# Local and global attention, then routed experts: the scores of a query block from one product of 160 columns on a reordered key buffer

## The chip, the cores and the metric

The kernel runs on one core of a Trainium2 chip. The metric is the device time of one execution in microseconds (us); lower is better. The core has TensorE (PE in the profile: matrix products, with weight loads, PEld, that overlap them), VectorE (DVE), ScalarE (ACT), GpSimd (POOL) and SyncE (SP). GpSimd and SyncE also issue DMAs, each in the order of its own program. Operands lie in SBUF, products land in PSUM, and a DMA moves data between DRAM and SBUF or within them.

## The reference

Batch 8, 8 heads, 512 local positions, 32 global ones, head size 64. A local query sees the 32 global keys and the local keys at most 32 positions away; a global query sees all 544 keys. The result, as 4352 tokens of 512, goes through eight experts, mixed by weights that are balanced in eight rounds.

```python
s_g = scale * np.matmul(q_g, k_all.transpose(0, 1, 3, 2))
out_g = np.matmul(sm(s_g), v_all)
s_ll = scale * np.matmul(q_l, k_l.transpose(0, 1, 3, 2))
mask = np.abs(pos[:, None] - pos[None, :]) <= window        # window = 32
s_ll = np.where(mask, s_ll, -1000000000.0)
s_lg = scale * np.matmul(q_l, k_g.transpose(0, 1, 3, 2))
a_l = sm(np.concatenate([s_lg, s_ll], axis=-1))
out_l = np.matmul(a_l, np.concatenate([v_g, v_l], axis=2))
...
for e in range(E):
    out += P[:, e:e + 1] * (np.maximum(x @ w1[e], 0.0) @ w2[e])
```

## The kernel before

The order of all instructions is written out by hand: each engine executes what the program gives it, in that order, and waits where an operand or a buffer is not ready.

**Units and steps.** A unit n is a pair of heads of one batch (n = 4 b + hp, 32 units). The loop over s (L516) runs 34 steps and works on several units at once. In step s stand, in this order: f1 (first-layer products of experts 0 and 1, `ph`, L475), st_B(s, 0), in even steps st_G1, st_D1(s-1), in odd steps st_G2, f2 (second layer, `py`, L489), st_D2, st_B(s, 1), two f1, st_B(s, 2), st_A(s+1), st_E(s-1), in odd steps st_G3, f2, st_G3n, every fourth step logits, f1. Up to step 6 the order differs a little, the expert products begin in step 5, and in steps 1 to 4 keep_busy (L505) puts products in that nobody reads. TensorE so has attention and expert products mixed in one stream.

**st_A** (L297) transposes the keys and queries of a pair of heads into two PSUM tiles (`pk`, `pq`, L305). VectorE copies the keys in natural order to kTe[n % 4] behind 32 zero columns (L307). ScalarE copies the queries to a block-diagonal tile, qbd (L314, two copies); the first six units (n < NPL) use a plain tile, qpl, instead.

**st_B** (L317) forms the scores of blocks of 64 queries for both heads at once: one product with 128 local keys (L337: 64 queries and 32 keys on each side) and one with the 32 global keys, kgT (L339), into 160 columns of a PSUM tile `sc`. VectorE adds the mask and takes the row extremum (L344), ScalarE the exponential (L347) into Pu.

**st_D1** and **st_D2** transpose the weights (ptw L354, tgx L364 and L368) and copy them out (pw by VectorE, pg and xT by ScalarE). **st_E** (L375) multiplies with the values: va and vb hold the local values at two offsets of 64 rows, vgz the global ones, four times, each for one place of the block in a group of four. VectorE divides (L392, L393).

**G1 to G3n** do the global queries, four heads at a time: G1 (L398) scores against the 512 local keys in kTe, in two products of 480 and 32 columns (because of where kTe ends), and against kgT, `sg`; G3 (L425) multiplies the weights with vb and, in a fifth product, with vgn, which holds the global values in its last 32 rows (L433). G3 of batch b runs in steps 4 b + 3 and 4 b + 5.

**Values.** load_v lets GpSimd load vg (to DRAM, L170), va (L171, L174) and a piece of vb. For the first two batches GpSimd copies va to vb (`part`); later, three DMAs on SP do (L191 to L193). load_vz (L159) then issues on SP four DMAs for vgz and one for vgn (L162) of the batch, from vg; vgz and vgn have two buffers each. For batch 0 load_vz stands ahead of step 0, for batch 1 in step 2 (L546), later in `move`. The wait for vg stands in the first of these DMAs; SP issues nothing behind it until it passes.

**PSUM.** `ph` and `py` share two buffers (ps_mm), `sc`, `pq` and `pl` two (ps_sc), the transposes and `pog` two (ps_tr), `po` and `sg` one (ps_po). The result of the second layer goes from `py` to yst by ScalarE (L492) and, when four are there, to DRAM by SP (L496).

After the loop come the balancing of the mixing weights, with expert products between, and experts 2 to 7 by a scheme of seven products for eight (L810, L908).

Of the kernel before, what the change touches and what calls it, by code (L numbers as in the profile page):

```python
# [23 lines left out]
def kernel(  # L24
# [31 lines left out]
    KW = P  # L56
    SW = KW + Sg
    VW = Dh + 1
    assert (B, H, Sl, Dh, Sg) == (8, 8, 512, 64, 32) and D == H * Dh and F % P == 0
    scale = 1.0 / float(Dh) ** 0.5  # L60

# [66 lines left out]
    with ExitStack() as att:  # L128
# [5 lines left out]
        ps_po = att.enter_context(tc.tile_pool(name="ps_po", bufs=1, space=PSUM))  # L134

        qpl = [att_c.tile([P, Sl], FP16, name=f"qpl{i}") for i in range(2)]
        mask = att_c.tile([P, 3, SW], FP32)
        kgT = att_c.tile([P, HP, B * Sg], FP16)
        qgT = att_c.tile([P, HP, B * Sg], FP16)
        qbd = [att_c.tile([P, NHB, P], FP16, name=f"qbd{i}") for i in range(2)]  # L140
        kTe = [att_c.tile([P, W + Sl + W], FP16, name=f"kTe{i}") for i in range(4)]
        vgr = [att_c.tile([P, 4 * H * VW], FP16, name=f"vgz{i}") for i in range(2)]
        vgz = [t.rearrange("p (a h v) -> p a h v", a=4, h=H) for t in vgr]
        vgn = [att_c.tile([P, H, VW], FP16, name=f"vgn{i}") for i in range(2)]
        own = att_c.tile([P, 4], FP16)
        vab = [(att_c.tile([P, NJ, H, VW], FP16, name=f"va{i}"),
                att_c.tile([P, NJ, H, VW], FP16, name=f"vb{i}")) for i in range(2)]
        xgn = [att_c.tile([P, D], FP16, name=f"xgn{i}") for i in range(2)]
        vg16 = [dscr.tile([Sg, H, Dh], FP16, name=f"vg16_{b}") for b in range(B)]

        staged = {}

# [6 lines left out]
        def load_vz(b):  # L159
            for i in range(4):  # L160
                nc.sync.dma_start(out=vgz[b % 2][i:P:4, i, :, 0:Dh], in_=vg16[b])
            nc.sync.dma_start(out=vgn[b % 2][P - Sg : P, :, 0:Dh], in_=vg16[b])  # L162

        def load_v(b):
            va, vb = vab[b % 2]
            vz = vgz[b % 2]
            src = v_l[b].rearrange("h s d -> s h d")

            def first():
                nc.gpsimd.dma_start(out=vg16[b], in_=v_g[b].rearrange("h g d -> g h d"))  # L170
                nc.gpsimd.dma_start(out=va[W:P, 0, :, 0:Dh], in_=src[0:96])  # L171

            def mid(j):
                nc.gpsimd.dma_start(out=va[:, j, :, 0:Dh], in_=src[P * j - W : P * j + 96])  # L174

            def last():
                nc.gpsimd.dma_start(out=vb[HB : HB + W, NJ - 1, :, 0:Dh], in_=src[Sl - W : Sl])

            def part(eng, lo):
                if lo:  # L180
                    eng.tensor_copy(out=vb[96:P, NJ - 1], in_=va[W : 2 * W, 0])
                    eng.tensor_copy(out=vb[0:HB, 0:2], in_=va[HB:P, 0:2])
                    eng.tensor_copy(out=vb[0:HB, 2:NJ], in_=va[HB:P, 2:NJ])
                else:
                    eng.tensor_copy(out=vb[HB:P, 0:2], in_=va[0:HB, 1:3])
                    eng.tensor_copy(out=vb[HB:P, 2], in_=va[0:HB, 3])

            def move():
                if b < 2:
                    return part  # L190
                nc.sync.dma_start(out=vb[96:P, NJ - 1], in_=va[W : 2 * W, 0])  # L191
                nc.sync.dma_start(out=vb[0:HB, :], in_=va[HB:P, :])
                nc.sync.dma_start(out=vb[HB:P, 0 : NJ - 1], in_=va[0:HB, 1:NJ])  # L193
                if b > 1:
                    load_vz(b)

            return [first] + [lambda j=j: mid(j) for j in range(1, NJ)] + [last, move]

# [61 lines left out]
        nc.scalar.activation(out=ones_f[:, 0:1], in_=ones_f[:, 0:1], func=AF.Exp, scale=0.0)  # L260
        nc.vector.memset(mask, 0.0)
        for t in (kTe[0], kTe[2], kTe[3]):
            nc.vector.memset(t[:, 0:W], 0.0)
            nc.vector.memset(t[:, W + Sl :], 0.0)

        def clear(i, eng):
            va, vb = vab[i]
# [4 lines left out]
        def clear_z(i, eng):  # L272
            eng.memset(vgr[i].bitcast(mybir.dt.uint32), 0)
            eng.tensor_copy(out=vgz[i][:, :, :, Dh], in_=own.unsqueeze(2).to_broadcast([P, 4, H]))
            eng.memset(vgn[i][0 : P - Sg], 0.0)
            eng.memset(vgn[i][P - Sg : P, :, Dh:VW], 1.0)

        clear(0, nc.vector)
        clear(1, nc.vector)
# [17 lines left out]
        def st_A(n):  # L297
            b, hp = divmod(n, HP)
            qs, ks = staged[b]
            qb, kt = qbd[n % 2], kTe[n % 4]  # L300
            pt = [ps_tr.tile([P, Sl], FP16, tag="tr", name="pk"), ps_sc.tile([P, Sl], FP16, tag="sc", name="pq")]
            for t, src in enumerate((ks, qs)):
                for so in range(NJ):
                    for a in range(2):
                        nc.tensor.transpose(pt[t][HB * a : HB * (a + 1), P * so : P * (so + 1)],  # L305
                                            src[:, 2 * hp + a, so, :], identity)
            nc.vector.tensor_copy(out=kt[:, W : W + Sl].rearrange("c (p s) -> c p s", s=NJ),  # L307
                                  in_=pt[0].rearrange("c (s p) -> c p s", s=NJ))
            if n < NPL:
                nc.scalar.copy(out=qpl[n % 2].rearrange("c (p s) -> c p s", s=NJ), in_=pt[1].rearrange("c (s p) -> c p s", s=NJ))  # L310
                return
            for a in range(2):
                r = slice(HB * a, HB * (a + 1))
                nc.scalar.copy(out=qb[r, :, HB * a : HB * (a + 1)].rearrange("c i (p s) -> c i p s", s=NJ),  # L314
                               in_=pt[1][r].rearrange("c (s i p) -> c i p s", s=NJ, i=NHB))

        def st_B(n, part):  # L317
# [10 lines left out]
            for ii in range(ni):  # L328
                i = i0 + ii
                if n < NPL:  # L330
                    for c0, c1, kk in ((0, KW, kt[:, HB * i : HB * i + KW]), (KW, SW, kgT[:, hp, Sg * b : Sg * (b + 1)])):
                        for a in range(2):
                            r = slice(HB * a, HB * (a + 1))
                            nc.tensor.matmul(sc[r, SW * ii + c0 : SW * ii + c1], qpl[n % 2][r, HB * i : HB * (i + 1)],
                                             kk[r], start=True, stop=True)
                    continue
                nc.tensor.matmul(sc[:, SW * ii : SW * ii + KW], qb[:, i, :],  # L337
                                 kt[:, HB * i : HB * i + KW], start=True, stop=True)
                nc.tensor.matmul(sc[:, SW * ii + KW : SW * (ii + 1)], qb[:, i, :],  # L339
                                 kgT[:, hp, Sg * b : Sg * (b + 1)], start=True, stop=True)  # L340
            for ii in range(ni):
                i = i0 + ii
                mi = 0 if i == 0 else (2 if i == NHB - 1 else 1)
                nc.vector.tensor_tensor_reduce(  # L344
                    out=ms[:, ii, :], in0=sc[:, SW * ii : SW * (ii + 1)], in1=mask[:, mi, :],
                    scale=-scale, scalar=BIG, op0=ALU.add, op1=ALU.min, accum_out=d["mx"][:, i : i + 1])
# [51 lines left out]
        def st_G1(b, g):  # L398
            n0 = HP * b + 2 * g
            gc = slice(Sg * b, Sg * (b + 1))  # L400
            sg = ps_po.tile([P, 2 * 512], FP32, tag="po")
            for c0, c1, k0 in ((0, Sl - W, 2 * W), (Sl - W, Sl, W), (Sl, S, None)):
                for hh in range(4):
                    pr, a = divmod(hh, 2)
                    r = slice(HB * a, HB * (a + 1))
                    rhs = kgT[r, 2 * g + pr, gc] if k0 is None else kTe[(n0 + pr) % 4][r, k0 : k0 + c1 - c0]
                    nc.tensor.matmul(sg[W * hh : W * (hh + 1), c0:c1], qgT[r, 2 * g + pr, gc], rhs, start=True, stop=True)  # L407
            m2 = att_wk.tile([P, 2], FP32, tag="m2")
            nc.vector.reduce_max(out=m2[:, 0:1], in_=sg[:, 0:S], axis=AX.X)
# [15 lines left out]
        def st_G3(b, g):  # L425
            pgs = gs.pop((b, g))
            va, vb = vab[b % 2]
            po = ps_tr.tile([P, 512], FP32, tag="tr", name="pog")
            for t in range(5):
                for par in range(2):  # L430
                    r, h0 = slice(HB * par, HB * (par + 1)), 4 * g + 2 * par
                    rhs = vb[:, t, h0 : h0 + 2, :] if t < NJ else vgn[b % 2][:, h0 : h0 + 2, :]
                    nc.tensor.matmul(po[r, 0 : 2 * VW], pgs[:, t, r], rhs, start=(t == 0), stop=(t == 4))  # L433
            gs[(b, g)] = po

# [74 lines left out]
        nc.vector.tensor_copy(out=mask[:, 2, 0:KW], in_=mask[:, 1, 0:KW])  # L510
        nc.vector.memset(mask[:, 0, 0:W], NEG)
        nc.vector.memset(mask[:, 2, 3 * W : KW], NEG)
        st_A(0)
        unread(2, 256)
        first_keys()
        for s in range(NU + 2):  # L516
# [41 lines left out]
            if s >= 6:  # L558
                k, hf = divmod(s - 6, 2)
                if k >= 1:  # L560
                    l2 = [((k - 1) % 2, (k - 1) // 2, 2 * hf + i) for i in range(2)]
            n1 = n2 = 0

            def f1(eng):
# [59 lines left out]
                st_G3n(gb, gg)  # L624
            if s >= 6 and (s - 6) % 4 == 0:
                logits(NJ * ((s - 6) // 4), NJ, ps_sc, "sc")
            if s == 8:
                transpose_g(1, "kgs")
                transpose_g(1, "qgs")
# [10 lines left out]

        def sk_max0():
            nc.vector.reduce_max(out=red[:, 0:1], in_=lg, axis=AX.XY)
            dg = att_wk.tile([P, P], FP32, tag="dg", bufs=1)
            nc.vector.tensor_scalar(out=dg, in0=identity, scalar1=red[:, 0:1], scalar2=None, op0=ALU.mult)
            pm = ps_po.tile([P, P], FP32, tag="po")
            nc.tensor.matmul(pm, ones_f, dg, start=True, stop=True)
# [443 lines left out]
```

## Time and profile before

| what | value |
|---|---|
| time, median of 3 runs | 998.37 us (997.82 to 999.82) |
| the profiled execution's own time | 998.93 us |
| its span, first to last instruction | 997.2 us |
| TensorE busy | 982.5 us, 99% of the span |
| VectorE, ScalarE, GpSimd busy | 767.2, 655.5, 301.7 us |
| granted TensorE clock, mean | 0.998 |
| scores of local blocks, one product with local and one with global keys each | 208 pairs in full width (units 6 to 31), 55 and 27 ns from start to start |
| one step of the loop from step 8 on | about 10.2 us |

All times in the views are microseconds from the span's start, durations of single instructions ns where said. A line of a timeline gives start, length, engine, line of the kernel, operation, destination and source, and in brackets idle time of the engine before it with what ended it. Merged lines (x8) cover several instructions, from the first start to the last end. SPq and POOL lines with DMA_DIRECT2D are issues; the time to landing is told apart. Ends of matmuls are modelled and overlap; their starts tell the rate.

### The profile page before, as it was taken

The numbers are of one execution on the slowest core, as the hardware profiler recorded it, in microseconds if no ns is written. First come the engines' busy times: TensorE is split into PE (matmuls) and PEld (weight loads), VectorE is DVE, ScalarE is ACT, GpSimd is POOL, SyncE is SP. The second block draws the span as 40 slices with busy tenths as digits, with TensorE's granted clock in tenths as the row PEclk, the third lists the DMA queues.
The fourth block names the chain that finished last, engine by engine and source line by source line (L and its number), as shares of the span: only waits on it lengthen the run. The fifth ranks groups of instructions, "written<-read, shape, count | busy, mean of one in ns | idle before, by whom it ended". The sixth has DMA issues, their size and how long they took to land.

```text
span 997.2 us, 22451 instructions
## 1 busy us (share of the span) xinstructions
PE 982.5 (99%) x8868; PEld 641.0 (64%) x8868; DVE 767.2 (77%) x1858; ACT 655.5 (66%) x1342; POOL 301.7 (30%) x364
## 2 busy tenths in 40 slices
PE   7899999999999999999999999999999999999998
PEld 4566566656665555666666666676767676776764
DVE  7866665666653755889999888997899999888885
ACT  6888888888884566765555555557765555555551
POOL 9748887888850102111111111111111111100000
PEclk9999999999999999999999999999999999999999
DMA  9999999999952387554543333575664543123043
GB/s 167 186 156 199 239 206 221 222 200 222 234 144 85 108 241 169 161 147 121 122 107 74 75 75 74 128 214 129 165 148 117 117 96 66 53 65 74 2 106 127
DMA packets 138058, 138.68 MB, mean 139 GB/s; under 512 B 56608, under 2 KB 110048, under 8 KB 135904
## 3 DMA queue, kind: packets, MB, share of 16 engines
q0 software_dynamic: 105696, 87.32, 49.6%
q1 hardware_dynamic: 31696, 49.60, 15.5%
q8 instruction: 69, 1.13, 0.5%
q10 hardware_dynamic: 560, 0.33, 0.1%
q14 instruction: 37, 0.30, 0.1%
HBM read 144.46 MB, written 39.58 MB: 185 GB/s over the span
## 4 chain that ended last, share of the span: by engine, by line
PE 94%; POOL 3%; DMA 1%; DVE 1%; issue 0%; SPq 0%; ACT 0%; POOLq 0%; DVEq 0%
PE z L810 30%; PE pa L908 18%; PE py L489 12%; PE ph L475 12%; PE pb L908 9%; PE pc L908 4%; PE po L388 1%; PE ptw L354 1%; PE zp L879 1%; PE sc L337 1%; DMA vgz<-vg 1%; PE pk L305 1%; PE tgx L364 1%; PE pq L305 1%; PE sg L407 0%; POOL va L174 0%
## 5 line engine op out<-in xcount | busy, mean ns | idle before, releaser
L810 PEld LDWEIGHTS <-hs 128*128 128x128 f16 x2264 | 220.7, 98 | 91.8 <-DVE hs L806 0.4
L810 PE MATMUL z<-w2e,hs 128*128 128x256 f16 x1304 | 195.6, 273 | 0.0
L810 PE MATMUL z<-v,hs 128*128 128x256 f16 x960 | 144.0, 273 | 0.0
L475 PE MATMUL ph<-xT,w1e 128*128 128x512 f16 (+1 forms) x576 | 129.3, 367 | 0.6 <-ACT xT L372 0.6
L347 ACT ACTIVATE Pu<-ms,mx 128x160 f16<-128x160 f32 x256 | 120.1, 636 | 13.3 <-DVE mx L344 10.4
L489 PE MATMUL py<-w2e,hT 128*128 128x512 f16 x544 | 128.2, 379 | 0.0
L831 ACT COPY z<-z 128x256 f32<-128x256 f32 x98 | 35.0, 357 | 141.7 <-PE z L810 141.7
L908 PEld LDWEIGHTS <-w1e 128*128 128x128 f16 x960 | 87.1, 98 | 51.6 <-issue 1.0
L908 PE MATMUL pa<-t,s 128*128 128x512 f16 x384 | 114.2, 379 | 0.0
L726 POOL DMA_DIRECT2D w1e<-in_moe_w_dram x24 | 17.5, 734 | 297.5 <-PE pa L908 220.4
L344 DVE CUSTOM_DVE_ANT_0 ms<-sc,mask 128x160 f32<-128x160 f32 x256 | 70.2, 320 | 46.6 <-ACT yst L492 30.0
L844 DVE SCALAR_TENSOR_TENSOR oy<-z,lg,oy 128x512 f32<-128x512 f32 x128 | 95.8, 749 | 7.6 <-ACT oy L849 5.1
L806 DVE TENSOR_TENSOR hs<-hs 128x512 f16<-128x512 f16 x224 | 94.9, 424 | 8.2
L912 DVE CUSTOM_DVE_ANT_0 hx<-pb,s 128x512 f16<-128x512 f32 x96 | 65.9, 687 | 36.4 <-ACT s L942 30.2
L726 POOL DMA_DIRECT2D w2e<-in_moe_w_dram x24 | 19.8, 833 | 243.6 <-PE z L810 214.2
L928 ACT ACTIVATE hs<-pa 128x512 f16<-128x512 f32 x96 | 57.2, 596 | 47.0 <-PE pa L908 46.9
L475 PEld LDWEIGHTS <-w1e 128*128 128x128 f16 x576 | 53.4, 98 | 52.9
L912 DVE CUSTOM_DVE_ANT_0 hs<-pb,s 128x512 f16<-128x512 f32 x96 | 65.9, 686 | 24.1 <-ACT s L942 23.7
L908 PEld LDWEIGHTS <-s 128*128 128x128 f16 x720 | 65.6, 98 | 28.5 <-issue 0.3
L489 PEld LDWEIGHTS <-hT 128*128 128x128 f16 x544 | 49.8, 98 | 51.9
L480 DVE TENSOR_SCALAR hT<-ph 128x512 f16<-128x512 f32 x58 | 40.1, 692 | 55.1 <-PE ph L475 55.0
L478 ACT ACTIVATE hT<-ph 128x512 f16<-128x512 f32 (+1 forms) x86 | 50.6, 588 | 28.8 <-PE ph L475 28.4
(197 smaller groups left out, 1971.0 us busy)
## 6 DMA issues: line engine op xcount, KB each, us to landing
ys<-yd SPq DMA_DIRECT2D x68, 256.0 KB, 3.2
yd<-yst SPq DMA_DIRECT2D x16, 1024.0 KB, 5.9
pw<-in_moe_w_dram POOLq DMA_DIRECT2D x24, 512.0 KB, 10.1
kept<-psum POOLq DMA_DIRECT2D x24, 512.0 KB, 5.3
s<-kept POOLq DMA_DIRECT2D x12, 768.0 KB, 8.9
v<-kept POOLq DMA_DIRECT2D x12, 768.0 KB, 8.9
w1e<-in_moe_w_dram POOLq DMA_DIRECT2D x12, 512.0 KB, 5.3
w2e<-in_moe_w_dram POOLq DMA_DIRECT2D x12, 512.0 KB, 6.7
```

The costliest lines, as they stand in the source:

```text
L344: nc.vector.tensor_tensor_reduce(out=ms[:, ii, :], in0=sc[:, SW * ii : SW * (ii + 1)], in1=mask[:, mi, :], scale=-scale, scalar=BIG, op0=A ...
L347: nc.scalar.activation(out=d["Pu"][:, i // 4, :, i % 4], in_=ms[:, ii, :], func=AF.Exp, scale=-1.0, bias=d["mx"][:, i : i + 1])
L475: nc.tensor.matmul(ph[:, 0:n], wts[e][0][:, dk, P * fm : P * (fm + 1)], xT[:, dk, c0 : c0 + n], start=(dk == 0), stop=(dk == DP - 1))
L478: nc.scalar.activation(out=hT[:, fm, 0:n], in_=ph[:, 0:n], func=AF.Relu)
L480: nc.vector.tensor_scalar(out=hT[:, fm, 0:n], in0=ph[:, 0:n], scalar1=0.0, scalar2=None, op0=ALU.max)
L489: nc.tensor.matmul(py, hT[:, fk, P * c : P * (c + 1)], wts[e][1][:, fk, :], start=(fk == 0), stop=(fk == FT - 1))
L806: nc.vector.tensor_tensor(out=o, in0=x, in1=y, op=op)
L810: nc.tensor.matmul(o, lhs[:, fk, :], rhs[:, fk, :], start=(first and fk == 0), stop=(fk == HF - 1), skip_group_check=True)
L844: nc.vector.scalar_tensor_tensor(out=o, in0=z, scalar=p, in1=o, op0=ALU.mult, op1=ALU.add)
L908: nc.tensor.matmul(o, lhs[:, dk, P * f : P * (f + 1)], rhs[:, dk], start=(first and n == 0 and dk == 0), stop=(dk == HD - 1), skip_group_c ...
L912: nc.vector._custom_dve(TENSOR_ADD_SAT, out=self.to(i, j), in0=self.of(ps), in1=self.of(s), s0=BIG, s1=0.0)
L928: nc.scalar.activation(out=self.to(1, 0), in_=self.of(self.pa), func=AF.Relu)
```

## The change

kTe becomes 24 chunks of 32 columns. From unit 6 on the keys stand in it in another order: for each group r of two blocks five chunks, with the odd-numbered chunks of keys, the even-numbered ones and, in the fifth, a copy of the global keys, such that the five chunks of an even block lie at every second chunk and those of an odd block side by side. VectorE writes this from PSUM in three copies in place of one (the last doubles the first chunk of keys at the end, where an odd block reads it and the mask hides it), and ScalarE copies the global keys in (k_global), ahead of the copies of the queries. st_B then needs one product of 160 columns; an odd block's keys come in the order 1, 3, 2, 4, so there is a permuted mask, and vb is loaded in that order. For the first two batches vb stays natural (GpSimd's copies), and the odd blocks of units 6 and 7 keep two products. st_G1 takes all local keys in one product from batch 2 on.

vgn becomes a single tile. Its load leaves load_vz: SP gets it in step 4 b + 2 of each batch, batch 0 too, behind what the step has put on SP's queue before. The four-DMA part of load_vz stays. The permuted masks are made by VectorE in step 7. dg loses its own buffer.

```diff
-        kTe = [att_c.tile([P, W + Sl + W], FP16, name=f"kTe{i}") for i in range(4)]
+        kTe = [att_c.tile([P, KC * W], FP16, name=f"kTe{i}") for i in range(4)]
-        vgn = [att_c.tile([P, H, VW], FP16, name=f"vgn{i}") for i in range(2)]
+        vgn = att_c.tile([P, H, VW], FP16)
+        def natural(b):
+            return b < 2
+        def k_block(n, i):
+            kt, r = kTe[n % 4], i // 2 * 5 * W
+            if i % 2:
+                return kt[:, r + 4 * W : r + 9 * W]
+            return kt[:, r : r + 9 * W].rearrange("c (k w) -> c k w", w=W)[:, 0:9:2]
+        def k_natural(n, i):
+            r = (i // 2 * 5 + 4) * W
+            return kTe[n % 4][:, r : r + 4 * W].rearrange("c (y x w) -> c x y w", x=2, w=W)
+        def k_global(n):
+            b, hp = divmod(n, HP)
+            kg = kTe[n % 4][:, 4 * W : 24 * W].rearrange("c (r k w) -> c r k w", k=5, w=W)[:, :, 4]
+            nc.scalar.copy(out=kg, in_=kgT[:, hp, Sg * b : Sg * (b + 1)].unsqueeze(1).to_broadcast([P, NJ, Sg]))
...
         def load_vz(b):
             for i in range(4):
                 nc.sync.dma_start(out=vgz[b % 2][i:P:4, i, :, 0:Dh], in_=vg16[b])
-            nc.sync.dma_start(out=vgn[b % 2][P - Sg : P, :, 0:Dh], in_=vg16[b])
...
-                nc.sync.dma_start(out=vb[0:HB, :], in_=va[HB:P, :])
-                nc.sync.dma_start(out=vb[HB:P, 0 : NJ - 1], in_=va[0:HB, 1:NJ])
+                nc.sync.dma_start(out=vb[0:W, :], in_=va[HB : HB + W, :])
+                nc.sync.dma_start(out=vb[HB : HB + W, :], in_=va[HB + W : P, :])
+                nc.sync.dma_start(out=vb[W:HB, 0 : NJ - 1], in_=va[0:W, 1:NJ])
+                nc.sync.dma_start(out=vb[HB + W : P, 0 : NJ - 1], in_=va[W:HB, 1:NJ])
...
-            nc.vector.tensor_copy(out=kt[:, W : W + Sl].rearrange("c (p s) -> c p s", s=NJ),
-                                  in_=pt[0].rearrange("c (s p) -> c p s", s=NJ))
+            kp = kt[:, W : W + Sl].rearrange("c (p s) -> c p s", s=NJ)
             if n < NPL:
+                nc.vector.tensor_copy(out=kp, in_=pt[0].rearrange("c (s p) -> c p s", s=NJ))
...
+            ko = pt[0].rearrange("c (s r h o p) -> c o r h p s", s=NJ, r=4, h=2, o=2)
+            for o in range(2):
+                kd = kt[:, (2 + 2 * o) * W : (22 + 2 * o) * W].rearrange("c (r k p s) -> c r k p s", r=4, k=5, s=NJ)
+                kd = kd[:, :, 0:2] if o else kd[:, :, 0:5:4]
+                nc.vector.tensor_copy(out=kd, in_=ko[:, o])
+            nc.vector.tensor_copy(out=kt[:, 22 * W : 23 * W].rearrange("c (p s) -> c p s", s=NJ), in_=ko[:, 0, 0, 0])
+            k_global(n)
...
-                nc.tensor.matmul(sc[:, SW * ii : SW * ii + KW], qb[:, i, :],
-                                 kt[:, HB * i : HB * i + KW], start=True, stop=True)
-                nc.tensor.matmul(sc[:, SW * ii + KW : SW * (ii + 1)], qb[:, i, :],
-                                 kgT[:, hp, Sg * b : Sg * (b + 1)], start=True, stop=True)
+                elif natural(b) and i % 2:
...
+                else:
+                    nc.tensor.matmul(sc[:, SW * ii : SW * (ii + 1)], qb[:, i, :], k_block(n, i), start=True, stop=True)
...
+            else:
+                cols = [(0, Sl, None)]
...
+            if s < NU and hp == 2:
+                nc.sync.dma_start(out=vgn[P - Sg : P, :, 0:Dh], in_=vg16[b])
...
+            if s == 7:
+                permuted_masks()
```

More of the change, by code (lines that the diff above doesn't have):

```diff
@@ L58 @@
     VW = Dh + 1
+    KC = 24
     assert (B, H, Sl, Dh, Sg) == (8, 8, 512, 64, 32) and D == H * Dh and F % P == 0
@@ L136 @@
         qpl = [att_c.tile([P, Sl], FP16, name=f"qpl{i}") for i in range(2)]
-        mask = att_c.tile([P, 3, SW], FP32)
+        mask = att_c.tile([P, 4, SW], FP32)
         kgT = att_c.tile([P, HP, B * Sg], FP16)
@@ L176, in last @@
             def last():
-                nc.gpsimd.dma_start(out=vb[HB : HB + W, NJ - 1, :, 0:Dh], in_=src[Sl - W : Sl])
+                r = HB if natural(b) else W
+                nc.gpsimd.dma_start(out=vb[r : r + W, NJ - 1, :, 0:Dh], in_=src[Sl - W : Sl])
             def part(eng, lo):
@@ L188, in move @@
             def move():
-                if b < 2:
+                if natural(b):
                     return part
                 nc.sync.dma_start(out=vb[96:P, NJ - 1], in_=va[W : 2 * W, 0])
-                nc.sync.dma_start(out=vb[0:HB, :], in_=va[HB:P, :])
-                nc.sync.dma_start(out=vb[HB:P, 0 : NJ - 1], in_=va[0:HB, 1:NJ])
-                if b > 1:
-                    load_vz(b)
+                nc.sync.dma_start(out=vb[0:W, :], in_=va[HB : HB + W, :])
+                nc.sync.dma_start(out=vb[HB : HB + W, :], in_=va[HB + W : P, :])
+                nc.sync.dma_start(out=vb[W:HB, 0 : NJ - 1], in_=va[0:W, 1:NJ])
+                nc.sync.dma_start(out=vb[HB + W : P, 0 : NJ - 1], in_=va[W:HB, 1:NJ])
+                load_vz(b)
             return [first] + [lambda j=j: mid(j) for j in range(1, NJ)] + [last, move]
@@ L262 @@
         for t in (kTe[0], kTe[2], kTe[3]):
-            nc.vector.memset(t[:, 0:W], 0.0)
-            nc.vector.memset(t[:, W + Sl :], 0.0)
+            nc.vector.memset(t[:, 0 : W], 0.0)
+            nc.vector.memset(t[:, W + Sl : 2 * W + Sl], 0.0)
         def clear(i, eng):
@@ L274, in clear_z @@
             eng.tensor_copy(out=vgz[i][:, :, :, Dh], in_=own.unsqueeze(2).to_broadcast([P, 4, H]))
-            eng.memset(vgn[i][0 : P - Sg], 0.0)
-            eng.memset(vgn[i][P - Sg : P, :, Dh:VW], 1.0)
+            if i == 0:
+                eng.memset(vgn[0 : P - Sg], 0.0)
+                eng.memset(vgn[P - Sg : P, :, Dh:VW], 1.0)
         clear(0, nc.vector)
@@ L335, in st_B @@
                                              kk[r], start=True, stop=True)
-                    continue
-                nc.tensor.matmul(sc[:, SW * ii : SW * ii + KW], qb[:, i, :],
-                                 kt[:, HB * i : HB * i + KW], start=True, stop=True)
-                nc.tensor.matmul(sc[:, SW * ii + KW : SW * (ii + 1)], qb[:, i, :],
-                                 kgT[:, hp, Sg * b : Sg * (b + 1)], start=True, stop=True)
+                elif natural(b) and i % 2:
+                    nc.tensor.matmul(sc[:, SW * ii : SW * ii + KW], qb[:, i, :], k_natural(n, i), start=True, stop=True)
+                    nc.tensor.matmul(sc[:, SW * ii + KW : SW * (ii + 1)], qb[:, i, :],
+                                     kgT[:, hp, Sg * b : Sg * (b + 1)], start=True, stop=True)
+                else:
+                    nc.tensor.matmul(sc[:, SW * ii : SW * (ii + 1)], qb[:, i, :], k_block(n, i), start=True, stop=True)
             for ii in range(ni):
                 i = i0 + ii
-                mi = 0 if i == 0 else (2 if i == NHB - 1 else 1)
+                mi = (0 if i == 0 else 2 if i == NHB - 1 else 1) if i % 2 == 0 or natural(b) else 2 if i == NHB - 1 else 3
                 nc.vector.tensor_tensor_reduce(
@@ L401, in st_G1 @@
             sg = ps_po.tile([P, 2 * 512], FP32, tag="po")
-            for c0, c1, k0 in ((0, Sl - W, 2 * W), (Sl - W, Sl, W), (Sl, S, None)):
+            if n0 < NPL:
+                cols = [(0, Sl - W, 2 * W), (Sl - W, Sl, W)]
+            elif natural(b):
+                cols = [(P * t, P * (t + 1), 2 * t + 1) for t in range(NJ)]
+            else:
+                cols = [(0, Sl, None)]
+            for c0, c1, k0 in cols + [(Sl, S, None)]:
                 for hh in range(4):
                     pr, a = divmod(hh, 2)
-                    r = slice(HB * a, HB * (a + 1))
-                    rhs = kgT[r, 2 * g + pr, gc] if k0 is None else kTe[(n0 + pr) % 4][r, k0 : k0 + c1 - c0]
+                    n, r = n0 + pr, slice(HB * a, HB * (a + 1))
+                    if c0 == Sl:
+                        rhs = kgT[r, 2 * g + pr, gc]
+                    elif n < NPL:
+                        rhs = kTe[n % 4][r, k0 : k0 + c1 - c0]
+                    elif natural(b):
+                        rhs = k_natural(n, k0)[r]
+                    else:
+                        rhs = kTe[n % 4][r, 4 * W : 24 * W].rearrange("c (t k) -> c t k", t=NJ)[:, :, 0:P]
                     nc.tensor.matmul(sg[W * hh : W * (hh + 1), c0:c1], qgT[r, 2 * g + pr, gc], rhs, start=True, stop=True)
@@ L431, in st_G3 @@
                     r, h0 = slice(HB * par, HB * (par + 1)), 4 * g + 2 * par
-                    rhs = vb[:, t, h0 : h0 + 2, :] if t < NJ else vgn[b % 2][:, h0 : h0 + 2, :]
+                    rhs = vb[:, t, h0 : h0 + 2, :] if t < NJ else vgn[:, h0 : h0 + 2, :]
                     nc.tensor.matmul(po[r, 0 : 2 * VW], pgs[:, t, r], rhs, start=(t == 0), stop=(t == 4))
@@ L512, with permuted_masks @@
         nc.vector.memset(mask[:, 2, 3 * W : KW], NEG)
+        def permuted_masks():
+            for i in (3, 2):
+                nc.vector.tensor_copy(out=mask[:, i, 0:KW].rearrange("q (y x w) -> q x y w", x=2, w=W),
+                                      in_=mask[:, 1, 0:KW].rearrange("q (x y w) -> q x y w", x=2, w=W))
+            nc.vector.memset(mask[:, 2, 3 * W : KW], NEG)
         st_A(0)
@@ L642, in sk_max0 @@
             nc.vector.reduce_max(out=red[:, 0:1], in_=lg, axis=AX.XY)
-            dg = att_wk.tile([P, P], FP32, tag="dg", bufs=1)
+            dg = att_wk.tile([P, 3, SW], FP32, tag="ms", name="dg")[:, 0, 0:P]
             nc.vector.tensor_scalar(out=dg, in0=identity, scalar1=red[:, 0:1], scalar2=None, op0=ALU.mult)
```

## The prediction

> **What bounds the kernel now.** I read the busy rows first, then the stretches of 25 us, then the timelines of each engine, in one steady step and in the first 50 us. The page and the stretches (columns: stretch, its length, busy time of PE, weight loads, VectorE, ScalarE, GpSimd, granted clock, DMA share, GB/s):
>
> ```profile
> PE 982.5 (99%) x8868; PEld 641.0 (64%) x8868; DVE 767.2 (77%) x1858; ACT 655.5 (66%) x1342; POOL 301.7 (30%) x364
> ...
> 0.00:25.00 25.00, 18.96 (x315) 11.98 (x317) 19.12 (x93) 17.09 (x37) 23.73 (x40) 0.93 1.42 167
> 25.00:50.00 25.00, 21.77 (x424) 14.80 (x423) 20.06 (x84) 21.99 (x51) 17.65 (x26) 1.00 1.55 186
> ...
> 200.00:225.00 25.00, 25.00 (x307) 14.90 (x305) 15.68 (x63) 20.64 (x45) 20.76 (x22) 1.00 1.17 202
> ```
>
> From about 53 us on TensorE never stops: every ns taken from its stream comes off the end, and every stall put into it is added. Only the first 50 us have holes, and there the chain of waits runs through GpSimd and its DMAs. So two places count: the steady step (some 10.2 us, steps 8 to 31) and the first steps.
>
> **The steady step.** Starts of matmuls on TensorE (start, length, engine, line, what), in step 21 and, the last two lines, in step 20:
>
> ```profile
> 192.40 0.22 PE L337 MATMUL sc<-kTe,qbd 128*128 128x128 f16 x1
> 192.45 0.18 PE L339 MATMUL sc<-kgT,qbd 128*128 128x32 f16 x1
> 192.48 0.22 PE L337 MATMUL sc<-kTe,qbd 128*128 128x128 f16 x1
> ...
> 187.74 0.18 PE L339 MATMUL sc<-kgT,qbd 128*128 128x32 f16 x1
> 187.85 0.41 PE L305 MATMUL pk<-identity,ks 128*64 128x128 f16 x8
> ```
>
> From start to start 128 columns take 55 ns and 32 columns 27 ns, 82 ns a block (eight 512-column products take 1.73 us, 216 ns each). One product of 160 columns: 216 x 160/512 = 68 ns, so 14 ns less. The last two lines show the exception: before work of another shape (transposes of 64 columns, or sg) the 32 columns take 107 ns; that is a drain, and a longer last product should wait it out just the same, 55 + 107 against 68 + about 94. I count nothing there (0 to 14 ns). Blocks that become one product: 26 units (6 to 31) x 8, less the 4 odd ones of units 6 and 7, is 200; 36 of them stand before such a change of shape (23 before the transposes of keys, 13 before sg). 164 x 14 ns = 2.3 us. The scores of the global queries (L407) go from 480 + 32 + 32 columns to 512 + 32: the four that run side by side take 217 instead of 204 ns and a group of 28 ns goes, 15 ns x 12 = 0.2 us. **TensorE: -2.5 us** (2.3 to 3.0).
>
> VectorE: one key copy becomes three. Copies of 512 strided fp16 from PSUM (L307) hold the engine 0.60 us, the 160-column reductions of L344 0.24, so about 1.04 ns a column plus 0.07; 256 + 256 + 32 columns make 0.77, so +0.17 us a step. After it VectorE idles 0.8 to 1.3 us before hT (L480) or lg (L464) in each steady step: hidden. If that cover were gone the hT copy would hold a ph buffer, 0.17 x 24 = 4 us. Units 6 and 7 and the permuted masks (two copies and a memset, 0.41 + 0.34 + 0.09 us by L509 to L512) fall into steps 5 to 7, where VectorE is nearly full: +0.4 us (0 to 1).
>
> ScalarE: the copy of global keys stands between Pu and qbd, and behind it wait the two qbd copies and yst:
>
> ```profile
> 189.53 1.28 ACT L314 COPY qbd<-pq 64x512 f16<-64x512 f16 x2
> 190.87 0.59 ACT L492 COPY yst<-py 128x512 f32<-128x512 f32 x1
> ...
> 190.67 1.89 PE L475 MATMUL ph<-xT,w1e 128*128 128x512 f16 x8
> ```
>
> The second ph tile of the last line (start 190.67 + 0.86 = 191.53) takes the PSUM buffer that yst frees at 191.46: 0.07 us of room, in every step. In front of yst there is 0.33 us in odd steps; in even ones ScalarE could have begun it about 0.15 us sooner (copies otherwise overlap by 0.1 us). Not shown in the trace: a copy of 128 columns. pg (256 columns) holds ScalarE 0.27 us and xT (512) 0.47, so about 0.16; a qbd copy (0.60) is the upper bound. At 0.16 it just fits, and I charge **+0.4 us** over the six even steps without logits; at 0.4 it is 1.4 us, at 0.6 some 6 x 0.4 + 12 x 0.2 = 5.
>
> SP: the moves of vb become four of 32 partitions (two more issues, some 0.6 us each); those of batch 5, issued from 169 us and landed with vgz at 183, are read at 198. Nothing.
>
> **The first steps: where the time will come from.** vgn, the global values for G3, becomes one tile, and its load moves from load_vz to step 2 of each batch, issued on SP *behind* load_vz(1). SP's queue before, and the product that reads vgn:
>
> ```profile
> 12.21 4.04 SPq L161 DMA_DIRECT2D vgz<-vg  x4
> 16.35 0.61 SPq L162 DMA_DIRECT2D vgn<-vg  x1
> 30.06 3.79 SPq L161 DMA_DIRECT2D vgz<-vg  x4
> 33.95 0.61 SPq L162 DMA_DIRECT2D vgn<-vg  x1
> ...
> 28.50 0.22 PE L433 MATMUL pog<-vgn,pgs 128*64 128x130 f16 x2
> ...
> DMA to landing us min/median/max: 10.9/10.9/10.9
> ```
>
> SP stands from 17 to 30.06, since the vgz loads of batch 1 wait for vg of batch 1 (issued by GpSimd at 21.55, landing 8.5 us later). Today batch 0's vgn went ahead, at 16.35. In the changed kernel SP's order is vgz(0) x4, vgz(1) x4, vgn(0): vgn(0) takes the place that vgn(1) has now, issue at 33.95, landing 10.9 us later (last fenced line: this one DMA, in a stretch in which the DMA engines are full) at 44.85. The product at 28.50 needs it, and behind it on TensorE waits everything. Resuming at 44.9: **16.4 us of stall**. Landings of such loads go from 4.3 to 10.9 us (median 5.9), so 9.8 to 16.4; I take 10.9, because it is the same place, size and neighbours (w1e, 1 MB, issued at 32.95, lands at 45.1).
>
> A sentence of the Trainium skill, DMA: Bandwidth & Descriptors, section "Anatomy of one DMA — SWDGE (gpsimd) path", puts most of a DMA at a constant of about 2 us; by that vgn would land at about 36 and the time would be about 1004. The rows of 4.3 to 10.9 disagree, so the sum goes by them.
>
> What the stall gives back: the wait on vgz(1) at 42.2 (0.8 us, the longest wait of these steps), and VectorE, which at 28.5 still has 0.85 us of the former product's work (L392, L393) to do, catches up, which removes the wait on pw (0.4) and about half of that on kTe (0.7): -1.6 us. What it costs more: TensorE's granted clock. After the hole from 9.4 to 10.78 the products ran at half speed to 14.2 (eight transposes of L354 took 1.04 us at 11.38, 0.65 at 17.47), and the first stretch's clock is 0.93. A hole of 16 us should end in 3.4 us at half speed: up to 1.7 us of work, partly under VectorE's; **+1.2** (0 to 3.4).
>
> The Trainium skill, TensorE: Matmul & The Clock Gate, section Part 1: The HAM clock gate (the "warmup" mystery), says that about 3.4 us without work halve the clock and about as long a busy window restores it. The 3.4 us at half speed of the trace agree.
>
> Later batches: vgn(b) waits for G3 of b-1, one step back, and is read two steps (20 us) after that: hidden even at 10.9 us.
>
> **Sum**, on the profiled execution (998.93 us, span 997.2): 16.4 - 1.6 + 1.2 + 0.4 - 2.5 + 0.4 = +14.3, 1013.2. That execution is 0.56 above the median of 998.37, so I predict **1012.7**.
>
> **Rivals.**
> (a) vgn lands earlier, at the median 5.9 or the least 4.3 us: stall 11.4 or 9.8, 1007.7 or 1006.1; at the 2.3 us of the quickest load of vg itself, the shortest of any global value, 1004.1 (chance 0.02 of its 0.13). For it: less traffic if GpSimd gets there sooner. Against: nothing there waits for TensorE.
> (b) The keys' copy on ScalarE takes 0.4 to 0.6 us, or waits, and yst is late in most steps: +0.6 to +4.6, 1013.3 to 1017.3. Against: 0.27 us for twice the columns.
> (c) The first steps don't stall, so not slower: vgn(0) lands before 28.5. SP needs 3.9 us from the first vgz to vgn and 4.3 for the landing, so vg(1) would have to be there by 20.3, before it is issued. Then 998.4 - 2.5 + 0.8 = 996.7, or 995.4 with nothing lost on the other engines. It is possible only if SP does not stay in order.
> (d) The 160 columns cost as much as both before (a strided read is slow): 2.5 us lost, 1015.2.
>
> **Chances.** Forecast 0.72 (its own range 1010.5 to 1015), (a) 0.13, (b) 0.07, (d) 0.05, (c) 0.03, half of that within 0.2% (about what a measurement of this kernel can tell from no change). Slower 0.97, same 0.015, faster 0.015. Range 1007 to 1016.5: the forecast, most of (a) and half of (b).
>
> **What would show it.** vgn's first issue on SP near 34 us, its landing near 45; one wait of TensorE of some 16 us at the product from vgn in G3, released by that DMA; half clock after it; sc products 68 ns apart; no idle time on TensorE in the steady steps, or a few tenths before ph. I am wrong if vgn(0) is issued before 30 us, or if idle time stands before ph in every step.

## The result and the profile after

The changed kernel takes 1013.34 us (median of 4 runs, 1011.68 to 1014.45) against 998.56 of the kernel before, run beside it: ratio 1.0147, 95% interval 1.0132 to 1.0163. 1012.7 was predicted. The profiled execution took 1013.21 us, its span is 1011.4.

The page and the stretches of the changed kernel, with the columns as in the prediction (the last four: GpSimd, granted clock, DMA share, GB/s):

```profile
PE 982.2 (97%) x8628; PEld 635.9 (63%) x8628; DVE 772.0 (76%) x1913; ACT 660.0 (65%) x1368; POOL 300.7 (30%) x362
...
PE   7389999999999999999999999999999999999998
...
PEclk9699999999999999999999999999999999999999
...
25.00:50.00 25.00, 8.92 (x146) 5.72 (x145) 7.12 (x33) 8.11 (x20) 16.96 (x25) 0.66 1.61 186
50.00:75.00 25.00, 21.78 (x386) 14.62 (x386) 19.11 (x84) 22.70 (x53) 10.38 (x14) 1.00 1.09 133
```

240 products fewer, TensorE's busy time nearly the same, and the span 14.2 us longer: the slices say where. The second one holds a hole on every engine but GpSimd, with the clock at 0.66; from the fourth on TensorE is full as before. SP's queue, the waits of TensorE (waiter, what it waited for, total, times, longest) and the product that waited:

```profile
12.14 21.03 SPq L180 DMA_DIRECT2D vgz<-vg  x8
33.21 0.74 SPq L611 DMA_DIRECT2D vgn<-vg  x1
```

```profile
PE pog L475 <- DMA vgn<-vg: 15.7, 1, 15.7
...
PE ph L517 <- ACT xT L401: 0.6, 1, 0.6
```

```profile
27.80 0.40 PE L475 MATMUL pog<-vb,pgs 128*64 128x130 f16 x8
43.90 0.32 PE L475 MATMUL pog<-vgn,pgs 128*64 128x130 f16 x2 [15.70 <-DMA vgn<-vg]
44.15 1.03 PE L547 MATMUL pm<-kTe,identity 128*128 128x512 f16 x2
```

The eight vgz loads of batches 0 and 1 now stand together (the second four wait until 29.9 for vg of batch 1), vgn's first load goes out behind them at 33.21, and G3 of batch 0 stops between its vb products and its vgn product. The chain of waits for the same stretch (start, length, what):

```profile
21.43 8.49 DMA vg<-in_v_g_dram
...
33.21 10.64 DMA vgn<-vg
...
43.90 0.32 PE pog L475 x2
```

To part the loss by stage I take the first transposes of steps 9 and 31 (ptw), before and after:

```profile
70.86 0.62 PE L354 MATMUL ptw<-identity,Pu 128*128 128x128 f16 x8
...
294.14 0.62 PE L354 MATMUL ptw<-identity,Pu 128*128 128x128 f16 x8
```

```profile
87.01 0.61 PE L383 MATMUL ptw<-identity,Pu 128*128 128x128 f16 x8
...
308.79 0.61 PE L383 MATMUL ptw<-identity,Pu 128*128 128x128 f16 x8
```

Up to step 9: +16.15 us. Steps 9 to 31: 221.78 against 223.28, -1.50 us. From there to the start of the last product: -0.1. Behind that product the changed kernel ends another 0.3 us sooner, which is why the span grows by 14.2 and the starts of products by 14.55; why that end is shorter is open.

### The profile page after: what moved, and what is told of

Same layout as the page of the kernel before. It is cut to its first block, busy times and chain, and to the rows that moved or that the text cites. A ratio compares the mean times of both kernels' runs of the same rounds, so it can differ in the third digit from the quotient of the medians.

```text
span 1011.4 us, 22059 instructions
## 1 busy us (share of the span) xinstructions
PE 982.2 (97%) x8628; PEld 635.9 (63%) x8628; DVE 772.0 (76%) x1913; ACT 660.0 (65%) x1368; POOL 300.7 (30%) x362
## 4 chain that ended last, share of the span: by engine, by line
PE 93%; DMA 2%; POOL 2%; DVE 2%; ACT 1%; issue 0%; SPq 0%; POOLq 0%; DVEq 0%; ACTq 0%
PE z L862 30%; PE pa L960 17%; PE py L531 12%; PE ph L517 11%; PE pb L960 9%; PE pc L960 4%; PE sc L369 1%; PE ptw L383 1%; PE po L417 1%; PE zp L931 1%; DMA vgn<-vg 1%; PE pk L326 1%; DMA vg<-in_v_g_dram 1%; PE tgx L393 1%; PE pq L326 1%
## 5 line engine op out<-in xcount | busy, mean ns | idle before, releaser
L376 ACT ACTIVATE Pu<-ms,mx 128x160 f16<-128x160 f32 x256 | 120.3, 635 | 13.0 <-DVE mx L373 10.9
```

Of the source, the lines that this page charges most:

```text
L376: nc.scalar.activation(out=d["Pu"][:, i // 4, :, i % 4], in_=ms[:, ii, :], func=AF.Exp, scale=-1.0, bias=d["mx"][:, i : i + 1])
```

## Experiments

**1. One DMA moved back.**

```diff
         load_vz(0)
+        nc.sync.dma_start(out=vgn[P - Sg : P, :, 0:Dh], in_=vg16[0])
...
-            if s < NU and hp == 2:
+            if 0 < b and s < NU and hp == 2:
```

> The changed kernel with one DMA moved back: the load of batch 0's vgn is issued on SP right behind the four vgz loads of batch 0, ahead of the vgz loads of batch 1; everything else as changed. Theory (the place of that load in SP's queue is the whole loss): issue near 16 us, no wait of TensorE at the vgn product, no half clock near 45 us, and a time some 16 us lower, 995.5 to 997.5, below the kernel before, since 2.5 us of products are saved. Rival (the new score path, with its copies on ScalarE and VectorE, costs part of it): above 999.

997.49 us against 999.56 (ratio 0.998, 0.9969 to 0.9992). SP's queue of this kernel:

```profile
15.89 0.61 SPq L314 DMA_DIRECT2D vgn<-vg  x1
29.75 4.04 SPq L180 DMA_DIRECT2D vgz<-vg  x4
```

The wait at the vgn product is gone and steps 9 to 31 take 221.79 us, as in the changed kernel. So the new score path gains about 2 us, and the place of one 32 KB load costs all of the loss. The single vgn tile is kept here, so that it has one buffer instead of two is not the cause.

**2. Only that DMA moved, in the kernel before.**

```diff
         def load_vz(b):
...
-            nc.sync.dma_start(out=vgn[b % 2][P - Sg : P, :, 0:Dh], in_=vg16[b])
+            if b > 1:
+                load_vn(b)
+        def load_vn(b):
+            nc.sync.dma_start(out=vgn[b % 2][P - Sg : P, :, 0:Dh], in_=vg16[b])
...
                     load_vz(1)
+                    load_vn(0)
+                    load_vn(1)
```

> The kernel before with that one DMA moved the other way: batch 0's vgn is issued on SP behind the four vgz loads of batch 1; scores, key buffer and copies as before. Theory: a wait of TensorE of 15 to 16.5 us at the vgn product of G3 and 4 to 5 us at half clock after it; 1013.5 to 1016. Rival (the rest of the change makes part of the loss): clearly under 1012.

1014.6 us against 999.56 (ratio 1.015, 1.013 to 1.0169), with the same hole and nothing else of the change. The longest wait of TensorE in this kernel:

```profile
PE pog L437 <- DMA vgn<-vg: 15.4, 1, 15.4
```

Experiments 1 and 2 are two halves of one proof: the load alone makes the loss, and without it there is none.

**3. TensorE kept at work during the wait** (70 products that nobody reads).

```diff
             for t in range(5):
+                if t == 4 and (b, g) == (0, 0):
+                    keep_busy(70)
```

> The changed kernel with 70 products of 512 columns that nobody reads in the place of the wait (between the vb products and the vgn product of batch 0's first G3): 70 x 0.216 = 15.1 us of work, a little less than the wait. It measures the price of the clock. If the half clock after the wait costs 1 to 2 us, as forecast, the time is 1 to 2 us lower, 1011.2 to 1012.3, with no stretch at half clock; if it is hidden by VectorE, no difference; if the products themselves delay anything, higher.

1012.24 us (ratio to before 1.0126, 1.0107 to 1.0145), 1.1 us under the changed kernel; but the two were timed in different rounds and the intervals of their ratios overlap, so the times alone don't settle the price. The traces do. The 70 products ended after the load had landed, so the vgn product ran at 44.45, 0.55 us later than in the changed kernel, yet step 9 begins earlier: from that product to the ptw of step 9 it takes 41.46 us, the changed kernel 43.11. The granted clock of the stretch 25 to 50 is 1.00 here:

```profile
25.00:50.00 25.00, 23.49 (x247) 12.74 (x247) 8.22 (x35) 9.04 (x22) 16.74 (x24) 1.00 1.60 185
```

So the half clock after the wait costs 1.65 us, by one profile of each kernel.

**4. Less traffic beside the load**: w1 of expert 1 (1 MB) issued later by GpSimd.

```diff
-                    queue += [lambda: wts.__setitem__(1, [load_w1(1)]), lambda: part(nc.gpsimd, True),
+                    queue += [lambda: part(nc.gpsimd, True),
...
-                    queue += [lambda: load_g(1, "kgs"), lambda: load_g(1, "qgs")]
+                    queue += [lambda: load_g(1, "kgs"), lambda: load_g(1, "qgs"),
+                              lambda: wts.__setitem__(1, [load_w1(1)])]
```

> The changed kernel with the load of experts' w1(1), 1 MB, issued by GpSimd some 8 us later (behind the global keys and queries). Theory (the late landing of vgn, 10.6 us, is traffic of the weight load beside it): vgn lands 4.5 to 6 us after its issue, the wait of TensorE is 9.5 to 11 us, the time 1007 to 1009. Rival (the landing is late because of the four vgz loads ahead of it in SP's own queue): still about 10 us, 1012.5 to 1014.

1009.01 us (ratio 1.0088, 1.0065 to 1.011). GpSimd came to that load at 47.4 instead of 32.4, so 15 us later and not 8. vgn was issued at 33.73 and landed 5.8 us later, behind the same four vgz loads; the longest wait of TensorE:

```profile
PE pog L475 <- DMA vgn<-vg: 9.1, 1, 9.1
```

The rival falls: the other 4.8 of the 10.6 us go with the weight load beside it. The time came out at the upper end of what was expected, the wait a little below.

**5. The copy of global keys behind yst**, with experiment 1's load. First what it is about. ScalarE and TensorE of the changed kernel at the end of an even step without logits:

```profile
244.33 1.01 ACT L376 ACTIVATE Pu<-ms,mx 128x160 f16<-128x160 f32 x2 [0.19 <-DVE mx L373]
245.09 0.36 ACT L168 COPY kTe<-kgT 128x128 f16<-128x128 f16 x1
245.35 1.18 ACT L342 COPY qbd<-pq 64x512 f16<-64x512 f16 x2
246.55 0.59 ACT L534 COPY yst<-py 128x512 f32<-128x512 f32 x1
```

```profile
246.22 2.00 PE L517 MATMUL ph<-xT,w1e 128*128 128x512 f16 x8
```

The copy holds ScalarE 0.26 us (245.09 to 245.35), yst ends at 247.14, and the fifth ph product, which needs its buffer, starts at 247.19 where 246.22 + 0.86 = 247.08 was due: the eight products last 2.00 instead of 1.89. Five such steps lie between steps 9 and 31. The list of waits has nothing of it, since the gap lies within the modelled ends of the products: it shows only in their starts.

```diff
-            k_global(n)
...
             f2("a")
+            if NPL <= s + 1 < NU:
+                k_global(s + 1)
```

> The kernel of e1 (vgn of batch 0 ahead) with ScalarE's copy of the global keys moved behind yst instead of ahead of the qbd copies. In the changed kernel this copy holds ScalarE 0.26 us and one ph product in each of five or six even steps starts 0.11 us late. Theory (the copy makes yst late, and yst holds the buffer of that ph tile): the late starts vanish and the steps 9 to 31 take 2.0 to 2.1 us less than before instead of 1.5; 0.5 to 0.6 us under e1, some 995.5 to 997. Rival (the late starts come from VectorE's three key copies): they stay.

996.97 us against 998.89 (ratio 0.9977, 0.9969 to 0.9986): this version beats both kernels. Steps 9 to 31 take 221.26 us, no ph product is late, and the three key copies of VectorE, still there, cost nothing:

```profile
70.96 0.61 PE L383 MATMUL ptw<-identity,Pu 128*128 128x128 f16 x8
...
292.21 0.61 PE L383 MATMUL ptw<-identity,Pu 128*128 128x128 f16 x8
```

**6. Two products again**, on the reordered buffer, with experiment 1's load.

```diff
-                    nc.tensor.matmul(sc[:, SW * ii : SW * (ii + 1)], qb[:, i, :], k_block(n, i), start=True, stop=True)
+                    kb = k_block(n, i)
+                    kb = kb[:, 0:KW] if i % 2 else kb[:, 0:4]
+                    nc.tensor.matmul(sc[:, SW * ii : SW * ii + KW], qb[:, i, :], kb, start=True, stop=True)
+                    nc.tensor.matmul(sc[:, SW * ii + KW : SW * (ii + 1)], qb[:, i, :],
+                                     kgT[:, hp, Sg * b : Sg * (b + 1)], start=True, stop=True)
```

> The kernel of e1 with two products a block again (128 local keys read from the reordered buffer, then 32 global keys from kgT); layout, key copies, the copy of the global keys and G1 as changed. It undoes only the merging. Theory (merging saves 13 to 14 ns a block, save ahead of a change of shape): steps 9 to 31 take 1.8 to 2.1 us longer than in e1, the whole about 2 to 2.3 us more, 998.5 to 1000. Rival (the second product was hidden): no difference.

999.42 us against 998.89 (ratio 1.0002, 0.9992 to 1.0011); steps 9 to 31 take 223.60, 1.81 more than in experiment 1. The merging is worth the 1.8 us at the lower end of what was worked out; without it the new layout leaves a small loss in these steps (223.60 against 223.28 before), in which five ph products start late again, by 0.09 us each.

**7. The copy of global keys on GpSimd**, with experiment 1's load.

```diff
-            nc.scalar.copy(out=kg, in_=kgT...
+            nc.gpsimd.tensor_copy(out=kg, in_=kgT...
```

> The kernel of e1 with the copy of the global keys made by GpSimd. If GpSimd, which executes loads and sums in order and waits in them, gets to it in time, the steps gain the same 0.5 us as with the copy behind yst; if it comes late, the sc products wait for it and steps 9 to 31 take longer than in e1 by some us. Neither theory of the main loss is touched: no wait at the vgn product.

1005.12 us (ratio 1.0063, 1.0047 to 1.0078): in steps 9 to 31 the first of the cases named happened, 221.25 us as in experiment 5. A copy that comes late happened too, but in step 6, where it had not been looked for: GpSimd came to its first copy, of unit 6, behind loads that wait for others, and TensorE stood:

```profile
50.52 0.58 POOL L225 DMA_DIRECT2D qgs<-in_q_g_dram  x1 [4.57 <-DMA w2e<-in_moe_w_dram]
51.14 0.29 POOL L168 COPY kTe<-kgT 128x128 f16<-128x128 f16 x1
```

```profile
PE sc L370 <- POOL kTe L168: 6.8, 1, 6.8
```

It is the main loss again, in little: work that is needed now, in the order of an engine that stands in somebody else's wait.

## Why the prediction was right, point by point

- **The place of vgn's load** (forecast: issue 33.95, landing 10.9 us later, stall 16.4). Measured: issue 33.21, landing 10.64, wait 15.7; the product ran 15.4 us later than before (43.90 against 28.50). Proved by experiments 1 and 2. That the landing would be late because of the weight load, and not early as in rival (a), was an argument from neighbours; experiment 4 shows it (5.8 us without that neighbour). Later loads of the same size in the changed kernel landed in 2.3 (issued at 58.7) to 9.2 us.
- **What the stall gives back** (forecast -1.6, with +0.4 for steps 5 to 7, and some -0.3 of products in steps 6 to 8). From the vgn product to step 9 it was 42.36 us before and 41.46 in experiment 3, which has the hole without the half clock: -0.9 in all where about -1.5 was forecast. VectorE's waits largely stayed: the changed kernel still shows 0.56 us for the keys at 50.47. The wait on vgz of 0.8 us is gone, but it is missing in experiment 1 as well, which has the new work and no hole and takes 42.02 us. So the hole itself gave back 42.02 - 41.46 = 0.56 us where 1.6 was forecast: this term is off by 1 us, as the stall is, the other way. The remaining 0.34 against before is not the merged product, since experiment 6 takes 42.01 with two products; how it parts between the missing wait and the work of steps 5 to 7 is open.
- **Half clock** (+1.2, bounds 0 to 3.4). Measured +1.65 (experiment 3): it lasted 4.7 us of work, not 3.4.
- **TensorE's products** (-2.5 over all steps). Starts stand 69 ns apart where 68 was forecast; ahead of another shape the wait is 162 ns against 55 + 107 before, so nothing is gained there, as charged. Three in a row in the changed kernel, from this line to the next one's start:

```profile
231.06 0.37 PE L369 MATMUL sc<-kTe,qbd 128*128 128x160 f16 x3
231.27 1.89 PE L517 MATMUL ph<-xT,w1e 128*128 128x512 f16 x8
```

  Experiment 5, where nothing is late, shows -2.02 us over the 22 steps from 9 to 31, that is 0.09 a step. Rival (d) falls.
- **ScalarE's copy** (+0.4 at 0.16 us a copy). Five late starts of 0.11 us make 0.55 in steps 9 to 31. The copy holds ScalarE 0.26 us, but what follows is delayed by the forecast 0.16: from the start of the two exponentials (Pu) to the end of the two qbd copies it takes 2.20 us in the changed kernel (244.33 to 246.53, in the lines of experiment 5) and 2.04 before (188.77 to 190.81), because the qbd copies behind it are 0.10 shorter, 1.18 instead of 1.28:

```profile
188.77 1.01 ACT L347 ACTIVATE Pu<-ms,mx 128x160 f16<-128x160 f32 x2 [0.24 <-DVE mx L344]
189.53 1.28 ACT L314 COPY qbd<-pq 64x512 f16<-64x512 f16 x2
```

  What was mis-sized is the room. Against the start of the ph products yst ends 0.13 us later than before (0.92 instead of 0.79), and of the 0.07 us counted as room 0.05 pass between the end of yst (247.14) and the start of the product that waits for it (247.19); 0.02 was left, and 0.11 of the 0.13 shows. The place (even steps without logits, at the buffer that yst frees) was right, and rival (b), late in most steps, falls: the odd steps have room.
- **VectorE's three copies** (hidden). They hold it 0.34 + 0.33 + 0.10 = 0.77 us against 0.60, as worked out; experiment 5 shows no cost.

The sum: +15.4 (stall), -0.9 +1.65 (up to step 9), -1.5 (steps 9 to 31), -0.1 after: +14.55 in the starts of TensorE's products, where +14.3 was forecast. The stall was 0.7 to 1 us shorter than its term and less came back behind it; the two errors nearly cancel. The path, the waits and their order were foreseen; that the total came out so close is in part luck.

## What to carry to other kernels

A load that moves in a queue takes over every wait that stands ahead of it there: before moving one, list what the queue waits for between the old place and the new one, and who needs the load first. A gain of 0.2% that is spread over some 200 products is easily hidden by one wait in the first steps; look at the start of the kernel by itself. The price of a late load also depends on what else is in flight, here 5.8 or 10.6 us for the same 32 KB.

## What the runs showed of the hardware that was not expected

The clock stayed at half longer than the 3.4 us of the prediction: in the changed kernel from 31.5, 3.3 us after the last product's end, to 48.6, 4.7 us after TensorE went on; in experiment 4 to 44.8, 5.2 us after; in experiment 2 to 50.3, 5.8 us after.

A copy on ScalarE took longer directly behind an exponential than behind another copy. The two qbd copies take 1.28 us behind Pu and 1.18 behind the copy of the global keys; that copy takes 0.36 us behind Pu and 0.30 behind yst. Experiment 5 has both at once, qbd behind Pu and the copy behind yst:

```profile
228.73 1.29 ACT L342 COPY qbd<-pq 64x512 f16<-64x512 f16 x2
...
230.54 0.30 ACT L168 COPY kTe<-kgT 128x128 f16<-128x128 f16 x1
```

Why is not shown. So a copy that is put between an exponential and another copy can cost less than the time for which it holds the engine, here 0.16 of 0.26 us.
